# Two-phase MoE routing on one TensorE core: the search split from the gathering of its rows, and stated two experts ahead

## The chip, the cores and the metric

The kernel runs on one core of a Trainium2 chip. The metric is the device time of one execution, in microseconds, the median of several runs; lower is better. The profile below is of one execution. Engines by their names in the profile: PE is the matrix engine (PEld its weight loads), DVE the vector engine, ACT the scalar engine, POOL the GpSimd engine, SP the queue that issues plain DMAs.

## What is computed

A windowed attention (4 batches, 8 heads, 576 positions, 64 dimensions a head) gives 2304 tokens of 512 values. Two mixture-of-experts layers follow, each with 8 experts of 512 x 1024 x 512. The first weighs all experts for each token. The second gives each expert at most `cap` = 288 tokens, greedily by logit, and this case is about it:

```python
logits = x @ w_gate
flat = logits.flatten()
order = np.argsort(-flat)
for idx in order:
    tok, e = (int(idx) // E, int(idx) % E)
    if assigned[tok] >= 0 or counts[e] >= cap:
        continue
    assigned[tok] = e
    counts[e] += 1
for e in range(E):
    mask = assigned == e
    h = np.maximum(x[mask] @ w1[e], 0.0)
    out[mask] = h @ w2[e]
```

## The kernel before

The attention and the first layer fill some 1590 us under an order written out by hand. The last 320 us are the second layer, and they lie outside that: a scheduler places each instruction on its engine's queue, by the order in which the code states it (earlier is more urgent) and by its own guess of durations. Each engine then runs its queue strictly in that order, so a wrong guess becomes a wait.

The second layer runs in eight phases, one for each expert in the order in which experts fill up. `route(ph)` (L1102) finds the phase's expert and tokens. Its search is a radix search for the logit at which the first expert is full: six rounds, each a comparison `G` on DVE (L1143, L1145), a histogram of 18 small matmuls (L1149), two short DVE reductions (`f8`, `fl`, L1151 and L1152) and one to three matmuls that broadcast the digit (L1156, `bs`). After it come the counts (L1168), the expert's index and the index `widx` of its weights (L1182), and the state that the next search needs: `ob`, `cap`, `un` (L1240 to L1246). Prefix sums give each token its slot (`tot`, L1211; prefix matmuls L1214 and L1216; `sl`, `jv`). One-hot rows `oh` and `rh` (L1230, L1234) and the index matmul (L1238, 18 matmuls) turn slots into the list of token rows `idx` (L1250). POOL gathers those rows from `xrows` in three parts of 96 (L1255), and the expert's weights in four parts of 1 MB (L1190). PE transposes the rows (L1274, three times 8), into `xgt`. The last phase has no radix search.

`ffn(ph)` (L1285) is the expert: 8 first-layer tiles of 12 matmuls with 288 columns each (L1299), evicted as `hh` on ACT (L1301) and `hl` on DVE (L1302), from two PSUM buffers, so a tile can start when the tile two before it has been evicted by both; then 4 second-layer tiles of 24 matmuls (L1311), evicted as `yT` (L1313). `put(ph)` (L1315) turns `yT` back (L1321), copies it on ACT into one of two tiles `tmp` (L1323) and scatters it to the output from POOL (L1325); its three parts stand inside the first layer of the next phase.

`second()` states the work in this order: the search and rows of phase 0, the rest of the first layer, then for each phase the whole of `route(ph + 1)` and `ffn(ph)`:

```python
bg.start("route", route_all())
for ph in range(E):
    bg.until(("r", min(ph + 1, E - 1)))
    ffn(ph, before)
    before = put(ph)
```

So `route(ph + 1)` runs inside `ffn(ph)`: its search beside the first layer, its rows and transposes beside the second. The tiles of a route have one buffer each, but for `widx` (2), `wp` (2), `idx` (3) and `sv` (3). The weights have two sets of buffers, used in turn, the gathered rows `xgb` six tiles, and `xgt` two.

## Time and profile before

| | us |
|---|---|
| median of 3 runs | 1925.43 |
| lowest and highest run | 1922.45, 1926.74 |
| time of the profiled execution | 1916.18 |
| its span, from first to last instruction | 1914.4 |
| PE busy in the span | 1845.1 |
| DVE busy | 1242.6 |
| ACT busy | 889.8 |
| POOL busy | 107.7 |

The profiled execution is 9.25 us shorter than the median of the runs. Busy time of PE holds the drain of each matmul, which overlaps the next one. A phase of the second layer is read from one first-layer start of `ffn` to the next: phase 0 from 1636.9 us, then 1665.8, 1700.9, 1735.95, 1771.0, 1806.0, 1841.0 and 1866.5. A wait is idle time of an engine just before an instruction, with what released it.

### The profile page before, as it was taken

How to read it: one execution, taken by the hardware profiler on the slowest of the kernel's cores; microseconds unless marked ns; L12 is line 12 of the kernel's file. 1: busy time of each engine (PE TensorE's matmuls, PEld its weight loads, DVE VectorE, ACT ScalarE, POOL GpSimd, SP SyncE). 2: the span in 40 equal slices, each digit the busy share in tenths (PEclk: the TensorE clock that was granted, in tenths of full speed). 3: DMA queues.
4: the chain of work that ended last, by engine and by line, in shares of the span. 5: the costliest groups of instructions: out<-in, count | busy, mean ns of one | idle time of the engine just before them, and what ended most of it. 6: DMA issues, size and time to landing. Idle time of an engine off the chain costs nothing.

```text
span 1914.4 us, 40759 instructions
## 1 busy us (share of the span) xinstructions
PE 1845.1 (96%) x16205; PEld 1319.9 (69%) x16205; DVE 1242.6 (65%) x3808; ACT 889.8 (46%) x2439; POOL 107.7 (6%) x140
## 2 busy tenths in 40 slices
PE   6999999999999999999999999999999998999987
PEld 5877555777676676767766867677677774667765
DVE  7777956664666666676667666766757767565540
ACT  6666334543455545555554555455534442222222
POOL 0000000000000000000000000000000102323231
PEclk8999999999999999999999999999999999899999
DMA  8573022320324225234351343234231111535451
GB/s 191 111 156 75 1 89 72 105 89 1 111 80 164 89 95 167 93 109 127 118 165 67 122 136 130 94 101 159 89 105 27 36 29 62 185 121 177 163 210 30
DMA packets 172799, 203.40 MB, mean 106 GB/s; under 512 B 83000, under 2 KB 130104, under 8 KB 168512
## 3 DMA queue, kind: packets, MB, share of 16 engines
q1 hardware_dynamic: 164928, 157.78, 27.1%
q0 software_dynamic: 7680, 43.02, 6.4%
q8 instruction: 127, 2.08, 0.4%
q14 instruction: 64, 0.52, 0.1%
HBM read 143.05 MB, written 57.71 MB: 105 GB/s over the span
## 4 chain that ended last, share of the span: by engine, by line
PE 74%; DVE 9%; DMA 7%; issue 5%; ACT 3%; POOL 1%; SPq 0%; POOLq 0%; ACTq 0%; DVEq 0%
PE p L940 27%; PE p L862 17%; PE pb L862 12%; PE p L770 4%; PE p L1299 4%; DMA ws<-st2k 2%; DMA raw<-in_moe_w_dram 2%; DVE st2k L347 1%; DMA raw<-xrows,idx 1%; PE pb L630 1%; DMA w2scr<-st2k 1%; PE pb L1149 1%; PE p L1311 1%; ACT st2k L345 1%; PE pb L617 1%
## 5 line engine op out<-in xcount | busy, mean ns | idle before, releaser
L940 PE MATMUL p<-w2b,hh 128*128 128x512 f16 x2304 | 686.1, 379 | 0.0
L940 PE MATMUL p<-w2b,hl 128*128 128x512 f16 x1152 | 436.6, 379 | 0.0
L940 PEld LDWEIGHTS <-hh 128*128 128x128 f16 x2304 | 221.6, 99 | 218.2 <-issue 0.7
L862 PEld LDWEIGHTS <-w1b 128*128 128x128 f16 x4032 | 340.3, 98 | 22.9 <-issue 4.2
L862 PEld LDWEIGHTS <-w1x 128*128 128x128 f16 x3024 | 256.2, 98 | 19.7 <-issue 5.9
L862 PE MATMUL p<-th,w1x 128*128 128x192 f16 x1344 | 221.3, 246 | 3.1 <-ACT sa L874 2.4
L862 PE MATMUL pb<-xh,w1b 128*128 128x192 f16 x1344 | 221.3, 246 | 0.0
L940 PEld LDWEIGHTS <-hl 128*128 128x128 f16 x1152 | 112.6, 98 | 135.4 <-issue 0.5
L862 PE MATMUL pb<-xl,w1b 128*128 128x192 f16 x672 | 165.3, 246 | 0.0
L862 PE MATMUL p<-tl,w1x 128*128 128x192 f16 x672 | 165.3, 246 | 0.0
L347 DVE SCALAR_TENSOR_TENSOR st2k<-raw,wsc,st2k 128x512 f16<-128x512 f32 x128 | 92.1, 748 | 49.9 <-ACT st2k L345 49.6
L956 DVE SCALAR_TENSOR_TENSOR acc<-p,SE,acc 128x512 f32<-128x512 f32 x126 | 94.0, 746 | 40.2 <-PE p L940 39.9
L345 ACT ACTIVATE st2k<-raw,wsc 128x512 f16<-128x512 f32 x128 | 87.0, 714 | 69.1 <-DMA ws<-st2k 54.8
L862 PE MATMUL p<-th,w1b 128*128 128x192 f16 x672 | 110.6, 246 | 3.0 <-ACT sc L895 2.9
L743 ACT ACTIVATE hh<-sb 128x192 f16<-128x192 f32 x168 | 61.0, 363 | 112.5 <-DVE sb L906 112.5
L1005 POOL TENSOR_TENSOR st2k<-tmp,st2k 128x512 f16<-128x512 f32 x18 | 24.5, 1361 | 1575.5 <-ACT tmp L1003 1554.6
L862 PE MATMUL pb<-xh,w1x 128*128 128x192 f16 x672 | 110.6, 246 | 0.0
L862 PE MATMUL p<-xh,w1b 128*128 128x192 f16 x672 | 110.6, 246 | 0.0
L743 ACT ACTIVATE hh<-sa 128x192 f16<-128x192 f32 x168 | 60.9, 363 | 106.4 <-DVE sa L880 106.4
L295 ACT ACTIVATE st2k<-raw 128x512 f16<-128x512 f32 x116 | 72.3, 624 | 80.4 <-DMA raw<-in_moe_w_dram 52.0
L744 DVE SCALAR_TENSOR_TENSOR hl<-sa,hh 128x192 f16<-128x192 f32 x168 | 60.2, 358 | 72.1 <-ACT hh L743 72.1
L744 DVE SCALAR_TENSOR_TENSOR hl<-sb,hh 128x192 f16<-128x192 f32 x168 | 60.1, 358 | 71.7 <-ACT hh L743 71.7
(308 smaller groups left out, 3280.9 us busy)
## 6 DMA issues: line engine op xcount, KB each, us to landing
raw<-in_moe_w_dram SPq DMA_DIRECT2D x128, 512.0 KB, 5.5
ws<-st2k SPq DMA_DIRECT2D x128, 256.0 KB, 4.4
w2b<-w2scr SPq DMA_DIRECT2D x28, 512.0 KB, 6.4
w2scr<-st2k SPq DMA_DIRECT2D x48, 256.0 KB, 4.3
xrows<-st2k SPq DMA_DIRECT2D x18, 257.0 KB, 3.1
vs<-in_v_dram SPq DMA_DIRECT2D x35, 128.0 KB, 4.1
ldq<-in_q_dram SPq DMA_DIRECT2D x16, 256.0 KB, 4.5
ldk<-in_k_dram SPq DMA_DIRECT2D x16, 256.0 KB, 4.8
```

The lines of the kernel that those rows point to most:

```text
L295: A.activation(junk[:, 0:512], s0, AF.Square, accum_out=mp[:, c:c + 1])
L345: A.activation(hi, src, AF.Copy, scale=sc)
L347: V.scalar_tensor_tensor(lo, src, sc, hi, op0=OP.mult, op1=OP.subtract)
L617: PE.transpose(pp[:, hp], pn[:, b, hp], ident)
L743: A.activation(hh[:, f, cols], src, AF.Relu)
L744: V.scalar_tensor_tensor(hl[:, f, cols], src, 0.0, hh[:, f, cols], op0=OP.max, op1=OP.subtract)
L770: PE.matmul(p[:, 0:w], w1v[wi][:, c, fs], x[:, c, ts], start=(n == 0), stop=(n == 3 * DC - 1))
L862: PE.matmul(bank[:, 0:HB], aq[wi][:, c, fs], xq[xi][:, c], start=(start and n == 0), stop=(n == 5), skip_group_check=True)
L940: PE.matmul(p, h[:, f, js], w2v[wi][:, f], start=(n == 0), stop=(n == 3 * FC - 1))
L956: V.scalar_tensor_tensor(acc[:, i], p, SE[:, e, i:i + 1], acc[:, i], op0=OP.mult, op1=OP.add)
L1005: G.tensor_tensor(xr[:, DM:2 * DM], xs, xr[:, 0:DM], OP.subtract)
L1299: PE.matmul(p[:, 0:CAP], wv1[f // 4][w][:, c, fs], xt[:, x * DC + c], start=(n == 0), stop=(n == 3 * DC - 1))
```

## The change

`route(ph)` now ends with the state: it no longer asks for weights and no longer builds `oh`, `rh`, `idx`, but states `ob`, `cap`, `un` and `wp` and returns a second generator, `rows_of(ph)`, with the slots `sl` and `jv` in hand. `rows_of` asks for the first half of the weights, builds `oh`, `ohj` and `rh`, runs the index matmul, gathers the rows, asks for the other half, and transposes. `weave(ph, b)` runs the search of phase `ph` and, from its second step on, one step of the rows part `b` of the phase before after each step of the search; what is left of `b` follows. Before `ffn(ph)` the code now states the search of `ph + 2` woven with the rows of `ph + 1`. `widx` and `wp` get three buffers, `sl` and `jv` two.

```diff
-        widx = rt([128, 1], "widx", I32, bufs=2)
+        widx = rt([128, 1], "widx", I32, bufs=3)
...
-        gather(*((0, x) for x in range(1 if ph == 0 else 2)))
...
-        sl = rt([128, NT], "sl")
+        sl = rt([128, NT], "sl", bufs=2)
...
-        oh = rc["oh"]
-        V.tensor_tensor(oh, ...)
-        ohj = rt([128, NT, NJ], "ohj")
-        V.tensor_tensor(ohj, ...)
-        rh = rt([128, NT, NJ, 2], "rh", F16)
-        V.tensor_tensor(rh, ...)
-        yield 1
-        pi = rc["psr"].tile([128, 512], F32, name="pb")
-        for t in range(NT):
-            PE.matmul(pi[0:R, 0:2 * NJ], oh[:, t], rh[:, t].rearrange("p j x -> p (j x)"), ...)
...
+        wp = rt([128, 1], "wp", bufs=3)
+        V.tensor_tensor(wp, wv[:, 0:1], wv[:, 1:2], OP.mult)
+        return rows_of(ph, last, sl, jv, wp, ws, widx)
+
+    def rows_of(ph, last, sl, jv, wp, ws, widx):
...
+        gather(*((0, x) for x in range(1 if ph == 0 else 2)))
+        oh = rc["oh"]
+        V.tensor_tensor(oh, ...)
+        ohj = rt([128, NT, NJ], "ohj")
+        V.tensor_tensor(ohj, ...)
+        rh = rt([128, NT, NJ, 2], "rh", F16)
+        yield 1
+        V.tensor_tensor(rh, ...)
+        yield 1
+        pi = rc["psr"].tile([128, 512], F32, name="pb")
+        for t in range(NT):
+            PE.matmul(pi[0:R, 0:2 * NJ], oh[:, t], rh[:, t].rearrange("p j x -> p (j x)"), ...)
...
+        def weave(ph, b):
+
+            a = route(ph)
+            n = 0
+            while True:
+                try:
+                    next(a)
+                except StopIteration as x:
+                    a = x.value
+                    break
+                n += 1
+                if b is not None and n > 1:
+                    next(b, None)
+            for _ in b or ():
+                pass
+            return a
...
+        b = weave(1, b)
         before = iter(())
         for ph in range(E):
-            bg.until(("r", min(ph + 1, E - 1)))
+            if ph + 2 < E:
+                b = weave(ph + 2, b)
+            elif b is not None:
+                for _ in b:
+                    pass
+                b = None
             ffn(ph, before)
```

In the new file lines 1205, 1207, 1251, 1256, 1260, 1264, 1269, 1246, 1282, 1307, 1309, 1310, 1319, 1321, 1329, 1331 and 1333 are what 1214, 1216, 1230, 1234, 1238, 1250, 1255, 1190, 1274, 1299, 1301, 1302, 1311, 1313, 1321, 1323 and 1325 were.

The first place is POOL's queue in phase 2, from the gather of the rows of phase 3 on. `raw` are the gathered rows, `w2b` and `xh` weight buffers, `out_0_dram` the output; the `idx` of a store tells its phase. Before (the rows of phase 3 are `idx_22166`, the stores of phase 1 `idx_21070`):

```order
L1325 DMA out_0_dram<-tmp_3046,idx_21070 2304x512 x3
L1190 DMA w1b_83<-ws00_120,widx_22105 128x4096
L1190 DMA w1b_83<-ws01_121,widx_22105 128x4096
L1255 DMA raw_78<-xrows_129,idx_22166 96x1028 x3
L1190 DMA w2b_84<-ws10_122,widx_22105 128x4096
L1190 DMA w2b_84<-ws11_123,widx_22105 128x4096
```

and now (the rows of phase 3 are `idx_22245`, the stores of phase 1 `idx_21149`):

```order
L1269 DMA raw_78<-xrows_129,idx_22245 96x1028 x3
L1246 DMA w2b_84<-ws10_122,widx_21857 128x4096
L1246 DMA w2b_84<-ws11_123,widx_21857 128x4096
L1333 DMA out_0_dram<-tmp_3046,idx_21149 2304x512 x3
L1246 DMA xh_75<-ws00_120,widx_22417 128x4096
L1246 DMA xh_75<-ws01_121,widx_22417 128x4096
```

The stores, which stood first in the phase, stand behind the row gathers and the second half of the weights, and the first half of the weights is that of phase 4 (`xh`) and not of phase 3.

The second place is ACT's queue in phase 2: `hh` are evictions of the first layer, `tmp` the three output copies of `put(1)`, `xgt` evictions of the row transposes. Before:

```order
L1301 ACTIVATE hh0_79<-p1_22213 128x288
L1323 ACTIVATE tmp_3046<-p2_22228,sv_21083 96x512
L1301 ACTIVATE hh0_79<-p1_22236 128x288
L1323 ACTIVATE tmp_3046<-p2_22251,sv_21083 96x512
L1301 ACTIVATE hh0_79<-p1_22259 128x288
L1323 ACTIVATE tmp_3046<-p2_22274,sv_21083 96x512
L1301 ACTIVATE hh0_79<-p1_22282 128x288
L1301 ACTIVATE hh0_79<-p1_22297 128x288
```

and now:

```order
L1331 ACTIVATE tmp_3046<-p2_22494,sv_21161 96x512
L1286 ACTIVATE xgt1_20238<-pb_22283 128x8x96
L1286 ACTIVATE xgt1_20238<-pb_22335 128x8x96
L1309 ACTIVATE hh0_79<-p1_22502 128x288
L1309 ACTIVATE hh0_79<-p1_22525 128x288
L1309 ACTIVATE hh0_79<-p1_22540 128x288
L1309 ACTIVATE hh0_79<-p1_22555 128x288
L1331 ACTIVATE tmp_3046<-p2_22517,sv_21161 96x512
L1309 ACTIVATE hh0_79<-p1_22570 128x288
L1309 ACTIVATE hh0_79<-p1_22585 128x288
```

The third output copy, which followed the third `hh`, follows the sixth, with two more behind it, and the evictions of the row transposes come into the first layer.

The third place is DVE's queue in phase 0, at the end of the search of phase 1: `oh` is the one-hot of the rows of phase 1, `un` and `hm` belong to the next search. Before (`p1_21162` is the fourth first-layer tile):

```order
L1302 SCALAR_TENSOR_TENSOR hl0_80<-p1_21162,hh0_79 128x288
L1228 SCALAR_TENSOR_TENSOR sl_21028<-jv_21034,sl_21028 128x18
L1232 TENSOR_TENSOR ohj_21039<-jv_21034,j3_20077 128x54
L1230 TENSOR_TENSOR oh_20240<-i96_20075,sl_21028 128x1728
L1234 TENSOR_TENSOR rh_21041<-ohj_21039,tp_20079 128x108
L1246 SCALAR_TENSOR_TENSOR un_20098<-s2_21030,un_20098 128x18
L1302 SCALAR_TENSOR_TENSOR hl0_80<-p1_21177,hh0_79 128x288
```

and now (`p1_21390` is the third tile, `p1_21405` the fourth):

```order
L1227 SCALAR_TENSOR_TENSOR un_20098<-s2_21028,un_20098 128x18
L1130 TENSOR_SCALAR mi_21063<-mi_21063 128x18
L1251 TENSOR_TENSOR oh_20240<-i96_20075,sl_21026 128x1728
L1132 SCALAR_TENSOR_TENSOR hm_21067<-sx_21061,un_20098 128x18
L1253 TENSOR_TENSOR ohj_21098<-jv_21032,j3_20077 128x54
L1133 TENSOR_SCALAR hm_21067<-hm_21067 128x18
L1310 SCALAR_TENSOR_TENSOR hl0_80<-p1_21390,hh0_79 128x288
L1143 TENSOR_TENSOR G_21071<-hm_21067,cj_20067 128x720
L1256 TENSOR_TENSOR rh_21100<-ohj_21098,tp_20079 128x108
L1310 SCALAR_TENSOR_TENSOR hl0_80<-p1_21405,hh0_79 128x288
```

The `hl` of the third and fourth tile stand behind `oh`, and the first `G` of the search of phase 2 with them.

On PE the row transposes and the index matmul of phase `ph + 1` stand in the first layer of `ffn(ph)`; they stood in its second layer.

## Rows read from the trace of the kernel before

**Rows 1.** Windows: length, busy us (count) of PE, PEld, DVE, ACT, POOL; PEclk; DMA

```profile
1636.90:1665.80 28.90, 28.05 (x241) 21.08 (x239) 14.73 (x66) 6.04 (x13) 6.90 (x7) 0.94 0.67 244
...
1735.95:1771.00 35.05, 33.46 (x372) 24.91 (x371) 21.19 (x83) 8.61 (x17) 9.85 (x10) 1.00 0.44 154
...
1841.00:1866.50 25.50, 22.27 (x187) 17.60 (x185) 7.76 (x21) 6.69 (x13) 7.46 (x8) 0.87 0.75 267
```

**Rows 2.** PE waits (us, times, longest): phase 3, then phases 0, 1, 5, 6

```profile
PE pb L1274 <- DMA raw<-xrows,idx: 1.1, 3, 0.4
PE pb L1238 <- DVE rh L1234: 0.3, 1, 0.3
PE pb L1214 <- DVE tot L1211: 0.2, 1, 0.2
...
PE pb L1274 <- DMA raw<-xrows,idx: 0.7, 2, 0.4
...
PE pb L1274 <- DMA raw<-xrows,idx: 2.0, 3, 1.2
...
PE pb L1274 <- DMA raw<-xrows,idx: 1.3, 3, 0.7
...
PE pb L1274 <- DMA raw<-xrows,idx: 3.0, 1, 3.0
```

**Rows 3.** PE timeline, end of phase 6's wait: start, us, line, op, count, [idle]

```profile
1855.88 0.82 PE L1274 MATMUL pb<-id,raw 96*128 96x96 f16 x8 [2.96 <-DMA raw<-xrows,idx]
1856.49 0.92 PE L1299 MATMUL p<-xgt,xh 128*128 128x288 f16 x3
...
1859.21 4.46 PE L1299 MATMUL p<-xgt,xh 128*128 128x288 f16 x24
```

**Rows 4.** PE timeline, phase 3

```profile
1744.91 0.60 PE L1321 MATMUL p<-ident,yT 128*96 128x128 f32 x4
1745.48 0.61 PE L1149 MATMUL pb<-A,G 128*40 128x8 f16 x18
1746.02 0.79 PE L1299 MATMUL p<-xgt,w1b 128*128 128x288 f16 x5
...
1762.14 0.97 PE L1238 MATMUL pb<-rh,oh 128*96 128x6 f16 x18 [0.30 <-DVE rh L1234]
...
1767.17 0.51 PE L1274 MATMUL pb<-id,raw 96*128 96x96 f16 x8 [0.36 <-DMA raw<-xrows,idx]
1767.53 0.29 PE L1311 MATMUL p<-hh,w2b 128*128 128x288 f16 x1
```

**Rows 5.** PE timeline, phase 0, after the prefix matmuls

```profile
1643.99 4.11 PE L1299 MATMUL p<-xgt,xh 128*128 128x288 f16 x32
```

**Rows 6.** POOL timeline, phase 3

```profile
1741.47 1.41 POOL L1325 DMA_INDIRECT out_dram<-tmp,idx  x1 [6.57 <-ACT tmp L1323]
1744.44 0.93 POOL L1325 DMA_INDIRECT out_dram<-tmp,idx  x1 [1.56 <-ACT tmp L1323]
...
1764.08 0.92 POOL L1255 DMA_INDIRECT raw<-xrows,idx  x1 [5.46 <-DVE idx L1250]
1765.31 0.92 POOL L1255 DMA_INDIRECT raw<-xrows,idx  x1 [0.30 <-issue]
```

**Rows 7.** DVE timeline, phase 3

```profile
1741.10 0.97 DVE L1145 SCALAR_TENSOR_TENSOR G<-hm,pb,cj 128x720 f16<-128x720 f32 x1 [0.57 <-PE pb L1156]
...
1763.65 0.16 DVE L1250 SCALAR_TENSOR_TENSOR idx<-ti 96x3 int32<-96x3 f32 x1
```

**Rows 8.** DVE timeline, phase 0

```profile
1645.97 0.45 DVE L1302 SCALAR_TENSOR_TENSOR hl<-p,hh 128x288 f16<-128x288 f32 x1
...
1646.54 1.95 DVE L1230 TENSOR_TENSOR oh<-i,sl 128x1728 f16<-128x1728 f16 x1
```

**Rows 9.** DMA issues from 1600 us on: count, KB each, median us to landing

```profile
out_dram<-tmp,idx POOLq DMA_INDIRECT x24, 2.7
...
w2b<-ws,widx POOLq DMA_INDIRECT x8, 8.1
```

More of the change, by code (lines that the diff above doesn't have):

```diff
@@ L1223, in route @@
             V.tensor_tensor(sl, sl, s2, OP.add)
-        jv = rt([128, NT], "jv")
+        jv = rt([128, NT], "jv", bufs=2)
         V.tensor_scalar(jv, sl, float(R), None, op0=OP.is_gt)
@@ L1246, in route, with rt, gather @@
             V.scalar_tensor_tensor(rc["un"], s2, 0.0, rc["un"], op0=OP.is_equal, op1=OP.mult)
+        wi = rt([128, 2, E], "wi")
+        wv = rt([128, 2], "wv")
+        V.tensor_tensor(wi, winv[:, 2:4], bc(eo[:, None, :], [128, 2, E]), OP.mult)
+        V.tensor_reduce(wv, wi, AX.X, OP.add)
+        wp = rt([128, 1], "wp", bufs=3)
+        V.tensor_tensor(wp, wv[:, 0:1], wv[:, 1:2], OP.mult)
+        return rows_of(ph, last, sl, jv, wp, ws, widx)
+    def rows_of(ph, last, sl, jv, wp, ws, widx):
+        def rt(shape, name, dt=F32, bufs=1):
+            return rc["rpool"].tile(shape, dt, name=name, bufs=bufs)
+        def gather(*parts):
+            with ExitStack() as st:
+                if "lastx" in rc:
+                    st.enter_context(tc.issue_after(rc["lastx"]))
+                for m, a in parts:
+                    G.indirect_dma_start(out=ws[m][:, a * 4096:(a + 1) * 4096], out_offset=None, in_=wscr[m][a],
+                                         in_offset=bass.IndirectOffsetOnAxis(ap=widx[:, :1], axis=0))
+        gather(*((0, x) for x in range(1 if ph == 0 else 2)))
+        oh = rc["oh"]
+        V.tensor_tensor(oh, bc(rc["i96"][:, None, :], [128, NT, R]), bc(sl[:, :, None], [128, NT, R]), OP.is_equal)
+        ohj = rt([128, NT, NJ], "ohj")
+        V.tensor_tensor(ohj, bc(jv[:, :, None], [128, NT, NJ]), bc(rc["j3"][:, None, :], [128, NT, NJ]), OP.is_equal)
+        rh = rt([128, NT, NJ, 2], "rh", F16)
+        yield 1
+        V.tensor_tensor(rh, bc(ohj[:, :, :, None], [128, NT, NJ, 2]), bc(rc["tp"][:, :, None, :], [128, NT, NJ, 2]), OP.mult)
+        yield 1
+        pi = rc["psr"].tile([128, 512], F32, name="pb")
+        for t in range(NT):
+            PE.matmul(pi[0:R, 0:2 * NJ], oh[:, t], rh[:, t].rearrange("p j x -> p (j x)"), start=(t == 0), stop=(t == NT - 1))
         ti = rt([R, NJ, 2], "ti")
@@ L1348, in second @@
             rc[n] = late.enter_context(tc.tile_pool(name=n, bufs=x, space=PSUM))
-        first = route(0)
-        for x in first:
+        def weave(ph, b):
[13 more added lines that the diff above has]
+            return a
+        b = weave(0, None)
+        for x in b:
             if x == "rows":
@@ L1354, in second @@
         rest()
-        def route_all():
-            for ph in range(E):
-                for _ in first if ph == 0 else route(ph):
-                    yield 1
-                bg.done.add(("r", ph))
-                yield 1
-        bg.start("route", route_all())
+        b = weave(1, b)
         before = iter(())
         for ph in range(E):
-            bg.until(("r", min(ph + 1, E - 1)))
+            if ph + 2 < E:
[4 more added lines that the diff above has]
+                b = None
             ffn(ph, before)
```

17 lines of the change are left out of this document (removed).

## Prediction

> **What bounds the kernel now.** I call the work between two first-layer starts of `ffn` phase 0 to 7. I read the trace in this order: the busy time by phase, the waits of PE in each phase, then the timelines of PE, POOL and DVE round those waits. [rows 1] In a middle phase PE is busy 33.46 of 35.05 us at full clock, DVE 21.19, POOL 9.85. So TensorE is the bound, and the same matmuls run in any order: an edit that moves no PE work out of the program can gain only PE's idle time. [rows 2] That is 1.1 + 0.3 + 0.2 = 1.6 us in phase 3, and phases 2 and 4 look the same; the transposes of the gathered rows (L1274) wait for their gather, the index matmul (L1238) for `rh`, the prefix matmul (L1214) for `tot`. The last two repeat in phases 1 and 5, the 0.3 in 6. Phase 0 has 0.7, phase 1 has 2.0 + 0.5 = 2.5, phase 5 has 1.3 + 0.5 = 1.8, phase 6 has 3.0 + 0.3 = 3.3.
>
> [...] All that can be won from phase 0 on is then 0.7 + 2.5 + 4.8 + 1.8 + 3.3 + 3.1 = 16.2 us.
>
> The stretch before phase 0 idles more, but there the order on PE and POOL stays as it is until the first L1299, so I count it at nothing.
>
> **The change part by part.** It adds no matmul and takes none away. `wp` and the three tiles with more buffers cost no instruction. The index and gather lines move from the end of a search into the next phase's first layer.
>
> *Phases 2 to 4: waits on `tot` and `rh`.* The prefix matmul stands in the second layer behind 30 first-layer matmuls, and `oh` and `rh` are made while the second layer runs, a third of a phase before the index matmul. Both waits go: 0.5 in each.
>
> *Phases 2 to 4: the wait on the gather.* Units, from start to start in [rows 4]: four `yT` transposes 0.57, a histogram of 18 matmuls 0.54, eight row transposes 0.36; a first-layer matmul 0.123, and an L1156 no more than that. From the end of the index matmul to the first transposes the new order has 19 first-layer matmuls, 7 `yT` transposes, one histogram and 5 L1156: 2.35 + 1.0 + 0.55 + 0.6, with switches about 4.6 us. The gather needs `ti` and `idx`, about 0.5 on DVE (0.7 in [rows 4, 7], where a `G` stands between), 0.27 from `idx` to POOL, and 3.09 from its start on POOL to the transposes [rows 4, 6, 7]: 3.9. The next two gathers start 1.22 apart [rows 6]. But it now starts while DVE runs the search's `G`, which it did not. [rows 6, 7] The store of 1741.47, which began 0.37 after a `G`, took 1.41 on POOL; the next, which began with none running, 0.93. I take 0.48 more for the first gather, and all three land that much later: 4.35, 5.57, 6.8 after the index matmul. PE asks at 4.6, then (eight transposes, two matmuls) at 5.25, then (eight transposes, a histogram, one matmul, after the 0.3 it waited) at 6.6. Waits 0 + 0.3 + 0.2 = 0.5 against 1.6.
>
> [...]
>
> *Phase 1* starts its index matmul 2.2 us later, with a fuller DVE: the same count gives 0.3 + 0.5 + 0.3 = 1.1 against 2.5.
>
> *Phases 5 and 6.* No full search is left, so less stands between the index matmul (now first in the phase) and the transposes: 12 + 9 matmuls and 4 `yT` transposes, 3.15 us, against 3.86 for the gather (no `G` beside it). Waits 0.7 + 0.5 + 0.4 = 1.6 in each, against 1.8 and 3.3. None is long, and three waits of this kind within 3 us left the clock full in phase 3 [rows 1, 2]: I take the 3.1 of lower clock as gone.
>
> *Phase 0 pays.* It takes over the second search's histograms, which phase 1 gives up: nothing by itself. But DVE's order there changes. `oh` starts at 1646.54 and holds DVE 1.9 us [rows 8]. Before, the `hl` of the third first-layer tile ran ahead of it; now it stands behind it and three short ones. That tile's PSUM buffer is what the fifth first-layer tile writes, so PE waits for it. PE: before, 32 first-layer matmuls follow the prefix matmuls from 1643.99 [rows 5]; now the prefix matmuls come two matmuls sooner, at 1643.7, and 23 matmuls, 2.8 us, stand between them and the fifth tile: it asks at 1646.5. DVE: `oh` starts no earlier (two more short ones ahead of it, one `hl` fewer), ends at 1648.4, then the short ones, 0.15, and the `hl` of 0.45 [rows 8]: 1649.0. A stall of 2.4 us, 1.9 to 3.0. The row gathers of that phase come out at 1.2, against 0.7.
>
> *Nothing at all:* the first-layer weights of the next phase but one are asked for when their buffer is free, a phase ahead (landing 8.1 us, [rows 9]); the index tile with three buffers waits for stores of two phases ago; the `sv` reads on DVE, which now stand inside the search, wait for the third gather and put the next step back 0.3, which PE covers with two matmuls and a `yT` transpose; without that cover it is 0.3 a phase.
>
> **Sum.** Before 16.2. After: phase 0 2.4 + 1.2, phase 1 1.1, phases 2 to 4 3 x 0.5, phases 5 and 6 2 x 1.6: 9.4. Gain 6.8, less 0.2 for the extra switches of PE between kinds of matmul: 6.6. The profiled execution goes from 1914.4 to 1907.8 of span, from 1916.18 to 1909.6 of time; the median of the runs lies 9.25 above that execution, and I carry the difference over: 1925.43 - 6.6 = **1918.8**, say 1919. About 0.2% (3.9 us) is what a measurement of this kernel can tell from no change.
>
> **Rivals.**
>
> [...]
>
> 2. *The gather waits stay.* PE's place for the transposes is fixed in the program; if the gathers land 0.3 later than I count, each of the three waits keeps its 0.3 in phases 1 to 4, a loss of 0.9 x 4 = 3.6: 1922.5. For it: in phase 1 before, one such wait was 1.2 [rows 2]. Against: no weights are in flight beside them any more.
>
> 3. *The stores fall behind the weights (slower).* In phases 2 to 6 the stores of the phase before stand on POOL behind three row gathers and two weight gathers. The third output copy on ACT needs the tile of the first store, and two `hh` of the first layer stand behind that copy on ACT. The first gather starts 4.6 us into the phase (3.8 for PE up to the end of the index matmul, 0.8 as above), and five issues of some 1.24 later store 0 starts, at 10.8. If it is not held up it lands 2.7 later [rows 9], at 13.5; if it lands with the weight gather issued at 9.6 (8.1 to land), at 18 to 19. The `hh` is wanted by the second layer at 22.9, so the copy may end as late as 22. It costs only if two such landings come one after the other, 9.6 + 16.2 + 2.7 = 28.5: 6 us in each of four phases, 24 - 6.6 more than before: 1943.
>
> [...]
>
> **How the numbers follow.** Forecast (1916.5 to 1921.5) 0.50; rivals 1 and 2 together 0.32, of which a third still ends under 1921.6; rival 4 0.08; rival 3 or another mishap of its sign 0.10. Faster by over 0.2%: 0.50 + 0.08 + 0.10 = 0.68; slower 0.10; within 0.2% 0.22. The range takes in rivals 1, 2 and 4, with the spread of the three medians' runs (3 below, 1.3 above): 1912 to 1925.5.
>
> **What would show it.** Right: in phases 2 to 4 no PE wait on `tot` or `rh`, and under 0.7 on the gathers; phase 6 without a 3 us wait, and the clock full there; in phase 0 one wait of about 2.4 on the DVE's `hl`, just before the fifth first-layer tile; phase 0 some 5 + 3 us longer, phases 5 and 6 shorter by as much as the search that they no longer hold. Wrong: a PE wait on ACT or on DVE inside the first layers of phases 2 to 4, ACT waiting for `out_dram`, a granted clock under 0.9 in phase 0, or transposes that still wait 1 us.

## The result: 1.3% slower on the recorded pair, level on two other chips

| | before | after |
|---|---|---|
| median of 4 runs each | 1923.94 us | 1947.27 us |
| lowest and highest run after | | 1944.66, 1949.49 us |
| ratio after to before, 95% interval | | 1.0129 (1.0102 to 1.0156) |
| time and span of the profiled execution | 1916.18, 1914.4 us | 1944.66, 1942.8 us |

Three of the four runs of before are those of the table ahead. The forecast was 1919 us and faster. The profile after, by phases 0, 3 and 6 (start to start of the first layer; columns as in [rows 1]):

```profile
1639.77:1680.29 40.52, 36.27 (x365) 26.00 (x364) 28.56 (x131) 6.02 (x13) 9.15 (x9) 0.90 0.48 176
1761.79:1802.00 40.21, 35.78 (x373) 26.66 (x371) 20.48 (x83) 8.37 (x17) 9.96 (x10) 0.92 0.39 135
1874.67:1903.93 29.26, 26.64 (x233) 20.89 (x231) 4.73 (x14) 7.62 (x16) 7.43 (x8) 1.00 0.34 113
```

A middle phase takes 40.2 us where it took 35.05 [rows 1], with the same matmuls. (The phase starts given ahead for the kernel before lie up to 1.45 us early: the first L1299 of phase 3 stands at 1737.40, not 1735.95. A middle phase is 35.06 us long by either, but phase 1 is 36.0 us and not 35.1.) PE's granted clock is 0.92 there: 1.00 up to 1773.8 us, 0.55 from there to 1778.0 and 0.50 in the 2 us after. PE's waits in phase 3 (us, times, longest) are not those of [rows 2]:

```profile
PE pb L1149 <- DVE G L1143: 2.0, 1, 2.0
PE pb L1149 <- issue: 1.1, 2, 0.5
PE pb L1156 <- issue: 0.5, 1, 0.5
PE pb L1282 <- issue: 0.5, 1, 0.5
PE pb L1282 <- ACT xgt L1286: 0.2, 1, 0.2
```

No wait on the gather, on `tot` or on `rh`. PE waits for the search's own `G`, and for nothing that the profile shows ("issue"). Why `G` is late stands on DVE. First PE's timeline of that stretch (start, us, line, count, [idle before]), then DVE's, then ACT's:

```profile
1767.30 0.61 PE L1149 MATMUL pb<-A,G 128*40 128x8 f16 x18
1769.06 0.16 PE L1156 MATMUL pb<-fl,sw 40*128 40x1 f16 x1 [0.47 <-issue]
...
1773.88 0.64 PE L1149 MATMUL pb<-A,G 128*40 128x8 f16 x10 [1.99 <-DVE G L1143]
1775.03 0.17 PE L1149 MATMUL pb<-A,G 128*40 128x8 f16 x1 [0.51 <-issue]
```

```profile
1768.66 0.16 DVE L1151 TENSOR_TENSOR f<-pb,cap 40x8 f32<-40x8 f32 x1 [1.49 <-PE p L1329]
...
1772.19 0.24 DVE L1160 TENSOR_SCALAR k<-hm,pb 128x18 f32<-128x18 f32 x1 [3.19 <-PE pb L1282]
...
1775.94 0.56 DVE L1284 COPY xgt<-pb 128x768 f16<-128x768 f16 x1 [1.99 <-remote]
```

```profile
1770.08 0.41 ACT L1309 ACTIVATE hh<-p 128x288 f16<-128x288 f32 x1 [3.55 <-PE p L1329]
```

The histogram of 1767.30 ended at 1767.91, but `f`, which reads it, starts 0.75 us later with DVE idle. The L1156 matmul of 1769.06 ended at 1769.22; `k`, which needs it, starts at 1772.19, 3.0 later; the `G` for which PE waits is made from `k`. The releasers that the profile names for them (L1329, L1282, "remote") are then only the last events that it has, not what the step waited for. In the trace of before the same two steps start 0.04 us behind their matmuls, as most do elsewhere in this trace (phase 3 of before, PE and then DVE):

```profile
1742.19 0.61 PE L1149 MATMUL pb<-A,G 128*40 128x8 f16 x18
1743.82 0.17 PE L1156 MATMUL pb<-fl,sw 40*128 40x1 f16 x1
```

```profile
1742.84 0.16 DVE L1151 TENSOR_TENSOR f<-pb,cap 40x8 f32<-40x8 f32 x1 [0.76 <-PE pb L1149]
...
1744.03 0.24 DVE L1160 TENSOR_SCALAR k<-hm,pb 128x18 f32<-128x18 f32 x1 [0.60 <-PE pb L1156]
```

I call this **late signals**: a step starts up to microseconds behind the end of the matmul that releases it, with its engine idle, as if the event came late. Only steps that wait for PE are so; DVE's `G` ends at 1773.82, and PE starts 0.06 us later. The same places are late in all middle phases, and PE stalls inside one histogram, as at 1775.03. The DMA view has a second mark of it: no time to landing for POOL's transfers, which [rows 9] had.

```profile
raw<-xrows,idx POOLq DMA_INDIRECT x24
out_dram<-tmp,idx POOLq DMA_INDIRECT x24
```

The weight gathers on that queue have none either. So the trace lacks landings of just POOL's queue, and signals are late while its row gathers run.

### The profile page after: what moved, and what is told of

It is laid out like the page before. It is cut to its first block, busy times and chain, and to the rows that moved or that the text cites. A ratio compares the mean times of both kernels' runs of the same rounds, so it can differ in the third digit from the quotient of the medians.

```text
span 1942.8 us, 40770 instructions
## 1 busy us (share of the span) xinstructions
PE 1853.8 (95%) x16205; PEld 1326.1 (68%) x16205; DVE 1239.4 (64%) x3808; ACT 887.7 (46%) x2439; POOL 109.5 (6%) x140
## 3 DMA queue, kind: packets, MB, share of 16 engines
q8 instruction: 127, 2.08, 0.4%
## 4 chain that ended last, share of the span: by engine, by line
PE 77%; DVE 9%; issue 5%; DMA 4%; ACT 3%; POOL 1%; another core or an unknown queue 1%; SPq 0%; POOLq 0%; ACTq 0%; DVEq 0%
PE p L940 30%; PE p L862 17%; PE pb L862 12%; PE p L770 4%; PE p L1307 3%; PE p L1319 3%; PE pb L1149 1%; DMA raw<-in_moe_w_dram 1%; DMA w2scr<-st2k 1%; PE pb L630 1%; DVE st2k L347 1%; PE pb L617 1%; PE pb L988 1%; PE pb L588 1%; DMA ws<-st2k 1%
## 5 line engine op out<-in xcount | busy, mean ns | idle before, releaser
L770 PE MATMUL p<-xh,w1b 128*128 128x384 f16 (+1 forms) x512 | 101.2, 288 | 6.0 <-DVE hl L752 5.8
```

What stands on the lines that cost most here:

```text
L770: PE.matmul(p[:, 0:w], w1v[wi][:, c, fs], x[:, c, ts], start=(n == 0), stop=(n == 3 * DC - 1))
```

## The experiments

Each run stands beside the kernel before on the same chip. The recorded pair's chip is not named. The runs fell on seven chips, each met on one occasion only, and on two of these, 0 and 13, signals were late.

| run | chip | median us | ratio to before, 95% interval |
|---|---|---|---|
| a_again, after unchanged | 4 | 1917.85 | 1.0011 (0.9992 to 1.0031) |
| a_third, after unchanged | 2 | 1920.78 | 1.0010 (0.9995 to 1.0026) |
| **a_fourth, after unchanged** | **0** | **1951.85** | **1.0111 (1.0084 to 1.0139)** |
| b_again, before unchanged | 15 | 1916.19 | 0.9996 (0.9985 to 1.0008) |
| b_bufs | 4 | 1913.78 | 0.9989 (0.9977 to 1.0001) |
| **b_shift64** | **0** | **1919.17** | **0.9949 (0.9925 to 0.9974)** |
| a_shift64 | 2 | 1910.14 | 0.9956 (0.9938 to 0.9973) |
| **a_shift128** | **0** | **1950.76** | **1.0109 (1.0084 to 1.0135)** |
| **a_shift64_oh** | **0** | **1948.79** | **1.0087 (1.0061 to 1.0113)** |
| a_shift64_oh2, the same | 11 | 1907.63 | 0.9954 (0.9938 to 0.9969) |
| rows_last | 4 | 1935.32 | 1.0095 (1.0078 to 1.0111) |
| rows_first | 4 | 1911.62 | 0.9985 (0.9970 to 1.0000) |
| rf_again, the same | 15 | 1913.98 | 0.9981 (0.9969 to 0.9993) |
| **rf_third, the same** | **13** | **1940.20** | **1.0084 (1.0060 to 1.0108)** |
| rf_shift64 | 1 | 1911.44 | 0.9974 (0.9964 to 0.9985) |
| a_svlate | 2 | 1922.74 | 1.0027 (1.0011 to 1.0042) |
| rf_svlate | 2 | 1915.48 | 0.9989 (0.9977 to 1.0001) |
| a_noxr | 15 | 1905.24 | 0.9943 (0.9923 to 0.9962) |

The rows in bold ran where signals were late. The kernel before itself took 1915.0 to 1918.1 on chips 1, 2, 4, 11 and 15, and 1928.9 and 1925.5 on 0 and 13. A theory's letter holds inside its own expectation.

### The program or the chip

Two theories for the late signals: they belong to the program (its order, or the addresses that the extra buffers moved), or to the load (the program as it was put on one chip at one time). The changed kernel again, without an edit, and the kernel before with the extra buffers alone:

```diff
+ widx, wp: bufs=3; sl, jv: bufs=2     (in the kernel before, nothing else)
```

> The changed kernel once more, for a second trace. In its first trace DVE and ACT start up to 5.2 us after the matmul that they wait for has ended (0.04 us everywhere else and in the kernel before), in a stretch of 8 us behind each row gather of phases 1 to 5, and PE then waits 2 to 5 us in the search and runs at the lower clock for some 5 us. Theory A, the late signals belong to the program: the same lags at the same places (0.75, 1.8, 2.3 to 3.0, 5.2 us in phases 3 to 5), time 1942 to 1950. Rival C, they are an accident of one load or one chip: other lags or none, and a time under 1935.

> The kernel before with the added buffers alone (widx and wp three, sl and jv two), which move the addresses of the tiles behind them and nothing else. Theory A (the late signals come from the search's steps standing beside the row gathers): as before, within 0.3%, no lag over 0.1 us behind the row gathers. Rival C (addresses or the program's place in memory make them): lags at the row gathers of phase 0, where the instructions of both kernels are the same and the changed one already shows 0.7 to 2.6 us, and 5 to 25 us slower.

> The changed kernel unchanged, a third time. Its first trace had late signals from PE behind the row gathers (up to 5.2 us) and was 1.3% slower than the kernel before; its second had none and was level with it (1917.9 against 1916.4). Theory C, the late signals belong to one load or one chip and not to the program: either kind may come, and with it the time: level within 0.3% without them, 1942 to 1950 with them. Theory A (they belong to the program) expects them each time and is already against the second trace.

> The changed kernel, unaltered, on one more load. If the late signals of the recorded run (k L1160 starting 3.0 us behind the end of its matmul in every middle phase, 1944.7 us) belong to the program, they are here again: 1942 to 1950. If they belong to that load or chip, as two loads without them suggest: 1914 to 1925 with every such lag at 0.04 us.

> The kernel before, unaltered, with a profile of its own on this load. If this load is of the kind that made PE's signals late under the changed kernel (a fourth of them: 1951.9 us against 1928.9 of before), theory L (during the row gathers' transfers the core's signals arrive late; the search's round trips between PE and DVE pay for it where they stand in that stretch) expects: the late starts are here too, but only at the two xgt copies behind the gathers, 2 to 2.5 us behind their transposes, with the search's k and f steps at 0.2 us or less, and middle phases of 35.0 to 35.5 us, 1917 to 1930 us in all. Rival A (the changed kernel alone makes signals late): no start later than 0.1 us and the gathers' landings complete in the record. On a load of the other kind: both at 1914 to 1920 with no late start.

On chips 4 and 2 the changed kernel is level with the kernel before, and no signal is late. In a_again, phase 3, the steps that were late stand so on DVE:

```profile
1750.12 0.16 DVE L1151 TENSOR_TENSOR f<-pb,cap 40x8 f32<-40x8 f32 x1 [0.78 <-PE pb L1149]
...
1750.92 0.24 DVE L1160 TENSOR_SCALAR k<-hm,pb 128x18 f32<-128x18 f32 x1 [0.45 <-PE pb L1156]
```

`k` starts 0.80 after `f`. In a_fourth, the same program on chip 0, 2.93 after it (phase 2):

```profile
1732.92 0.16 DVE L1151 TENSOR_TENSOR f<-pb,cap 40x8 f32<-40x8 f32 x1 [1.52 <-PE p L1329]
...
1735.85 0.24 DVE L1160 TENSOR_SCALAR k<-hm,pb 128x18 f32<-128x18 f32 x1 [2.58 <-PE pb L1282]
...
1740.32 0.56 DVE L1284 COPY xgt<-pb 128x768 f16<-128x768 f16 x1 [2.71 <-remote]
```

with ACT's `hh` between them, and ACT's copy of the row transposes 5.3 us behind those, which ended at 1734.93:

```profile
1734.36 0.41 ACT L1309 ACTIVATE hh<-p 128x288 f16<-128x288 f32 x1 [3.60 <-PE p L1329]
...
1740.21 0.81 ACT L1286 ACTIVATE xgt<-pb 128x768 f16<-128x768 f16 x1 [3.60 <-remote]
```

```profile
1734.42 0.51 PE L1282 MATMUL pb<-id,raw 96*128 96x96 f16 x8
```

Where signals are late, they come to DVE and ACT in bursts: here at 1732.92, 1734.36, 1735.85 and 1740.2, in phase 3 of the recorded trace at 1768.66, 1770.08, 1772.19 and 1775.84, so with no one spacing. That goes from about 2 us after the first row gather begins on POOL (1730.09 in this phase, 1765.86 in the other) to some 10 us after; behind the start of a store at 1683.41 us of the recorded trace, with no row gather near, an `f` starts 0.35 and a `G` 0.20 us behind the end of its matmuls. All four traces from chip 0 show it, and no trace from chips 1, 2, 4, 11 and 15. So it is the chip, or the occasion, that makes signals late: no chip was met twice, and these two were not told apart. The program decides what that costs: 1.1% here, by an order that is level elsewhere. Addresses alone do not make signals late, since a_again and a_fourth are one program; and b_shift64 (below) has late signals without the extra buffers. b_bufs ran where nothing was late, and shows only that the buffers cost nothing there.

### What late signals cost in the order before

The kernel before with 64 tiny matmuls in its first microseconds (meant for the next section) fell on chip 0, and is the only trace of the order before from such a chip.

```diff
+ for _ in range(64):
+     PE.matmul(pp[0:2, 0:2], pad, pad, start=True, stop=True)
```

> The kernel before with the same 64 tiny matmuls (128 PE instructions). If theory E is right the gain of 0.5% with 64 in the changed kernel belongs to the meeting of its gathers with the fetch: the kernel before, whose middle phases show no gather landing 4.5 us after its issue, stays within 0.2% of itself (ratio 0.998 to 1.002), and the changed kernel with the shift is then faster than the kernel before by the change itself. Rival: the shift alone is worth 0.4 to 0.5% in any kernel: ratio 0.995 to 0.996, and the change is worth nothing.

Its ratio is the rival's, and the kernel before left no trace on that chip to set beside it. What its trace does show is where late signals fall (its line numbers are 5 higher than before's): phase 3, and from the end of phase 2 DVE's copy of the row transposes and PE's first histogram of the next search.

```profile
1741.74:1776.94 35.20, 33.47 (x373) 24.92 (x370) 21.09 (x83) 8.67 (x18) 9.86 (x10) 1.00 0.45 156
```

```profile
1740.60 0.56 DVE L1281 COPY xgt<-pb 128x768 f16<-128x768 f16 x1 [2.77 <-PE p L1316]
```

```profile
1741.19 0.61 PE L1154 MATMUL pb<-A,G 128*40 128x8 f16 x18
```

The copy starts 2.4 us behind its transposes, which end at 1738.20. But the copy is wanted by the next phase's first layer only, so nobody waits, and a phase takes 35.2 us at full clock, as in [rows 1]. The search starts at 1741.19, when the gathers are over. In the changed kernel the search's rounds, in which PE, DVE and PE wait for each other in turn, stand in that very stretch. From the start of phase 0 to the end a_fourth takes 309.5 us against 280.8 in a_again, 28.7 more; b_shift64 takes 283.4 against 275.8 in b_again, 7.5 more: 4.5, 4.4 and 2.1 in phases 0, 5 and 6 (in 0 and 6 PE does wait for ACT's copy of the transposes, 2.0 and 3.4 us), less 3.4 in phase 1, which is the fetch's (below). The difference, 21 us, is 1.1%. These are single executions on four loads, so the 21 us are an estimate.

The next runs were to test that with the search behind the rows:

```diff
-                b = weave(ph + 2, b)
+                for _ in b:
+                    pass
+                b = weave(ph + 2, None)
```

> The run of before with the next phase's rows stated whole ahead of the search two phases ahead (1911.6 us, ratio 0.9985, where signals were on time). On a load with late signals theory L expects it level with the kernel before, 0.995 to 1.003, since its search's round trips stand behind the row gathers as they do before, with k starting within 0.5 us of its matmul's end; the interleaving of the rows with the search is then what costs the changed kernel its 1.1 to 1.3% on such a load. Rival P (going two phases ahead costs by itself there): 1.008 to 1.014. On a load of the other kind: 0.997 to 1.000 again.

> The next phase's rows stated whole ahead of the search two phases ahead, on one more load. If its signals are late (landings of POOL's queue missing from the record): theory L, 0.995 to 1.003 of before with k starting within 0.5 us of its matmul's end; rival P, 1.008 to 1.014. If its signals are on time: 0.997 to 1.000 as in the two runs so far, which then stand as one result over three loads.

rf_again fell on a chip without late signals and repeats rows_first. rf_third fell on chip 13, and its 1.0084 is the rival's number. The trace says why my number was wrong. Phase 3, and DVE in it:

```profile
1761.12:1799.97 38.85, 34.89 (x373) 26.47 (x371) 21.09 (x83) 8.49 (x17) 9.75 (x10) 0.96 0.40 140
```

```profile
1764.81 0.16 DVE L1151 TENSOR_TENSOR f<-pb,cap 40x8 f32<-40x8 f32 x1 [1.91 <-PE p L1307]
...
1767.01 0.97 DVE L1145 SCALAR_TENSOR_TENSOR G<-hm,pb,cj 128x720 f16<-128x720 f32 x1 [1.55 <-PE pb L1282]
```

Stated behind the rows, the search still does not run behind them: its second round's `f` and third round's `G` fall beside the gathers and start 1.2 and 1.4 us behind their matmuls, which ended at 1763.62 and 1765.61. `k`, which I had named, falls after the stretch and is on time. So the run had not the property that it was to test. What it shows is that the same order loses 5.5 us a phase against rf_again (38.85 against 33.33), with all of PE's longer waits in the stretch of late signals. That the rival (going two phases ahead costs by itself) is wrong is supported by the 0.998 of that order elsewhere, not by a run that separates the two on such a chip.

Which transfers make signals late was the question of a_noxr: the changed kernel without the row gathers of phases 2 to 7, which work on rows gathered by phases 0 and 1.

```diff
+            if ph < 2:
                 xd = G.indirect_dma_start(out=x, ...)
```

> The changed kernel without the row gathers of phases 2 to 7 (they work on rows that phases 0 and 1 gathered; the rest of the work, the weight gathers and the stores stay). On a load with late signals, theory R (the row gathers' transfers make them late): no late start of f, k, hh or xgt in the phases from the third on, phases 2 to 5 at 33 to 34 us where the changed kernel has 40 to 42, 1915 to 1925 in all. Rival W (the weight gathers or the stores of POOL's queue make them late): late starts of 2 us and more stay in phases 2 to 5 and it stays over 1935. On a load of the other kind: the gather waits of phases 2 to 6 and the half clock behind them go, 1902 to 1909.

It fell on a chip without late signals, so the run does not answer it. The trace of the recorded pair answers a part: later in phase 3, with no row gather near them, a store (1787.76) and both weight gathers start on POOL, and ACT's evictions of the second layer stay 2.94 us apart, the first of them 0.04 us behind its matmuls.

```profile
1789.20 1.21 POOL L1246 DMA_INDIRECT w1b<-ws,widx  x1 [0.30 <-issue]
1790.72 1.10 POOL L1246 DMA_INDIRECT w1b<-ws,widx  x1 [0.30 <-issue]
```

```profile
1792.75 0.41 ACT L1321 ACTIVATE yT<-p 128x288 f32<-128x288 f32 x1 [2.89 <-PE p L1319]
1795.69 0.41 ACT L1321 ACTIVATE yT<-p 128x288 f32<-128x288 f32 x1 [2.53 <-PE p L1319]
```

So weight gathers alone do not make signals late; that row gathers alone do is not shown. a_noxr gives a price instead, the middle phase with no row gather at all:

```profile
1746.79:1779.84 33.05, 33.00 (x375) 25.53 (x373) 20.68 (x84) 8.61 (x18) 7.14 (x7) 1.00 0.42 146
```

PE is busy 33.00 of 33.05 us: on such chips everything that the changed order still loses in middle phases is the gathers' waits and the clock behind them. 1905 us, with no row gather from phase 2 on, is about its floor.

### PE's instruction fetch in the gather's way

Where signals were on time, phases 2 to 4 had one gather wait of 0.7 to 1.8 us each, where I had forecast small ones of 0.5 in all. a_again, phase 3: POOL's second row gather, PE, and the DMA traffic between 1750.9 and 1752.6 us (the row of a queue: packets, MB, share of 16 engines).

```profile
1749.26 0.92 POOL L1269 DMA_INDIRECT raw<-xrows,idx  x1 [0.30 <-issue]
```

```profile
1753.89 0.51 PE L1282 MATMUL pb<-id,raw 96*128 96x96 f16 x8 [1.33 <-DMA raw<-xrows,idx]
```

```profile
q8 instruction: 1, 0.02, 4.9%
```

The gather took 4.6 us from issue to use where the median of this trace's 24 row gathers is 3.1 us to landing; 15 of its 16 landings came by 1752.32, the last at 1753.85. q8 carries instructions, in pieces of 16 KB (its row for the whole execution of a_again: 127 packets, 2.08 MB). That they are PE's is my inference: PE has 32410 instructions with its weight loads, and 2.08 MB over these is 64 bytes each. Here one piece goes through amid the gather's packets (4.9% of 16 engines over 1.7 us is 1.3 us of one engine). In each of the phases 2 to 4 of a_again, a_third and a_svlate a fetch starts 2.6 to 5.4 us behind the first gather. The kernel before has the same once, in phase 1: a fetch starts 4.1 us behind the first gather of its profiled execution (4.8 in b_again), the third gather is used 4.0 (5.0) us after its issue, and PE waits 1.2 (2.2) us for it. To move the fetch, I put 64 tiny matmuls (128 PE instructions with their weight loads, half a piece) into the first microseconds; with 128 of them a whole piece, so that the fetch should fall back where it was.

> The changed kernel with 64 tiny extra matmuls (128 instructions with their weight loads) on PE in the first 5 us, while it waits for its first input; they write nothing that is read. In the second trace of the changed kernel a 16 KB instruction fetch of PE (queue q8) started at 1751.1, among the packets of the second row gather of phase 3, one of the 16 engines landed that gather 1.5 us after the other 15, and PE waited 1.3 for it; phases 2 and 4 have the same. Theory E (the fetch holds up that one engine's rows): the extra instructions move the fetch half a page, some 5 us in that stretch, out of the gathers of phases 2 to 4; the waits there fall from 1.3 to 1.5 to under 0.5 each, the 3.4 us of lower clock in phase 4 go, and the time is 4 to 6 us less than the changed kernel's, 1911 to 1914 where the changed one has 1918. Rival F (the gather is late for another reason, such as the G beside it): waits of 1.3 stay and the time is the changed kernel's within 2 us.

> The changed kernel with 128 tiny matmuls in its first microseconds (256 PE instructions, one whole 16 KB page of them, where the run with 64 had half a page); their outcome is used by nothing. Theory E (PE's 16 KB instruction fetch falls amid the row gather's packets and holds its last landing): with a whole page added the fetch falls back where it was among the instructions, so the gather waits of phases 2 to 4 return at 1.2 to 1.5 us each, with half clock behind one or two of them: 1916 to 1922 us, level with the unchanged changed kernel. Rival (the tiny matmuls help by something else, such as an earlier clock or a later start of PE): no gather wait over 0.4 us in phases 2 to 4 and 1909 to 1912 us, as with 64.

> The next phase's rows stated whole ahead of the search two phases ahead, and 64 tiny matmuls (half a page of PE instructions) in the first microseconds. On a load with signals on time: theory E gives no more here, since with the rows whole the middle phases already show gather waits of 0.2 to 0.3 us, so it is level with the rows stated whole alone (0.998 to 1.000 of before); rival: the shift is worth its 0.5% in any order of statement, 0.993 to 0.995. On a load with late signals theory L (the search's round trips pay where they stand beside the row gathers) gives 0.990 to 1.003 of before with k starting within 0.5 us of its matmul's end; rival P (going two phases ahead costs by itself there) 1.006 to 1.014.

a_shift64: 10.6 us less than a_third on the same chip. Between the two traces 8.2 us lie from phase 0 on: 2.9 in phase 0, 7.1 in phases 2 to 4, and 1.7 lost again in 5 and 6; 2.5 us lie ahead of phase 0, where the fetch theory names nothing. No gather wait in phases 0 to 4, no fetch in the 5 us behind a first gather in phases 1 to 4, and the phase is near a_noxr's floor:

```profile
1740.54:1773.71 33.17, 33.03 (x373) 25.32 (x371) 20.59 (x83) 8.41 (x17) 10.70 (x10) 1.00 0.47 164
```

a_shift64_oh2 (below) repeats that on another chip. a_shift128 fell on chip 0, where late signals cover what it was to show: its fetches are back, 2.6 and 2.9 us behind the first gathers of phases 2 and 3, but its time says nothing on them, and the rival (the tiny matmuls help by something else) is not excluded by a run. rf_shift64 gains nothing over rows_first and rf_again beyond their intervals, as expected: that order has no such wait to lose. b_shift64's 0.5% on chip 0 speaks against "it is worth nothing in the order before". A part of it is the fetch of phase 1, which moved to 1.2 us ahead of the first gather: the phase takes 35.1 us at full clock where b_again has 38.5 at 0.96. The rest is not explained. The order before with the 64 matmuls did not run on a chip without late signals, so it is not shown that the changed order adds anything to them.

PE itself has no wait of the kind "issue" in phases 0 to 6 of a_again; what the fetch costs there is the gather's, 1.5 us of landing.

### The wide comparison beside POOL

Phase 5 had gather waits of 2.9 us where 1.6 were forecast. a_again, POOL and then DVE at its start:

```profile
1815.68 2.63 POOL L1269 DMA_INDIRECT raw<-xrows,idx  x1 [11.19 <-DVE ohj L1253]
1818.61 0.92 POOL L1269 DMA_INDIRECT raw<-xrows,idx  x1 [0.30 <-issue]
```

```profile
1815.56 1.95 DVE L1251 TENSOR_TENSOR oh<-i,sl 128x1728 f16<-128x1728 f16 x1
```

The first gather begins 0.12 us after the last phase's `oh`, an instruction with two SBUF inputs, and takes 2.63 us instead of 0.92: it ends 0.8 after `oh` does. A weight gather that begins at 1751.70, 0.06 behind a `G` of 0.91 us with two SBUF inputs (L1143), takes 1.68 and ends 0.8 after it. In rows_last (below) the second gather of phase 3 begins 0.36 us after an `oh` and takes 2.40. Where the gather began first it was not held (0.92 at 1748.03 in phase 3, with a `G` from 1748.37). The edit queues that `oh` behind the three `sv` products on DVE, on top of a_shift64:

```diff
+            if last:
+                st.enter_context(tc.issue_after(rc["lastsv"]))
             V.tensor_tensor(oh, ...)
```

> The run with 64 tiny matmuls, and in the last phase's rows the wide one-hot comparison (L1251 of the changed kernel, 1.95 us of DVE) is queued on DVE behind the three sv products of the rows before, so it no longer runs while POOL begins phase 5's first row gather. Theory (a POOL DMA issue that begins while a wide DVE instruction with two SBUF inputs runs is held until that ends): the first gather of phase 5 takes 0.9 to 1.0 us on POOL instead of 2.6, PE's gather wait there falls from 2.5 to 0.6 to 1.0 us and its half clock of some 3.4 us goes: 2 to 3.5 us less than with 64 alone, 1906.5 to 1908.5. Rival (the first gather is late by something else, the fetch or its own list): it still takes 2.6 us and the time stays at 1909 to 1911.

> The run with 64 tiny matmuls and the last phase's wide one-hot comparison behind the three sv products, once more, since its first run fell on the load with late signals. On a load with signals on time: the first row gather of phase 5 at 0.9 to 1.0 us on POOL, PE's wait there at 0.6 to 1.2 us and its half clock gone, 1906 to 1909 us or 0.993 to 0.996 of before (0.9956 with the 64 alone); rival (the wait there is the landing's, whoever issues it): 1909 to 1912, 0.995 to 0.997. On a load with late signals: 1.006 to 1.012 again.

The first gather of phase 5 takes 0.93 on chip 0 and 0.92 on chip 11:

```profile
1806.86 0.92 POOL L1277 DMA_INDIRECT raw<-xrows,idx  x1 [10.82 <-DVE ohj L1261]
...
1813.04 2.62 POOL L1342 DMA_INDIRECT out_dram<-tmp,idx  x1 [0.31 <-issue]
```

```profile
1812.91 1.94 DVE L1259 TENSOR_TENSOR oh<-i,sl 128x1728 f16<-128x1728 f16 x1
```

Phase 5 goes from 33.0 to 30.2 us with the clock full, as forecast. But the moved `oh` now holds a store, and phase 6 grows from 29.6 to 32.3, with an `hl` wait of 2.6 and a clock of 0.95; that the store is the reason is not shown. The ratio is a_shift64's. What held the gather is shown; the time gained by it is not.

### The rows' place, and the `sv` products

rows_last states the search two phases ahead whole and the rows behind it; rows_first the other way round (its diff stands above).

```diff
-                b = weave(ph + 2, b)
+                nb = weave(ph + 2, None)
+                for _ in b:
+                    pass
+                b = nb
```

> The changed kernel with the weaving undone inside the loop: the search of two phases ahead is stated whole, and the rows part of the next phase behind it, so that rows, gathers and transposes come after the search's rounds again while the search stays two phases ahead. Theory A: no histogram stands beside a row gather any more, so the lags go, the clock stays full, 1915 to 1928. Rival B (the search two phases ahead is what costs, by the later stores, weights and copies): 1940 to 1950 still. Rival C: lags stay behind the gathers, over 1935.

> The changed kernel with the rows part stated whole ahead of the search of two phases ahead: index matmul, gathers and transposes first in the phase, the search behind them in urgency but at the same time where its own chain lets it. Theory A: the histograms still run while the gathers are in flight, so the lags stay, perhaps shorter by what the first rounds lose: 1935 to 1950, PE idle 3 to 5 us in phases 2 to 4. Rival D (it is the sv reads and transposes queued inside the search on DVE and PE that hold it up, not the late signals): the search no longer has them between its steps, so the wait for G falls under 0.5 us and the time under 1928.

rows_last misses the numbers of A and B, and has the time of C without its lags (no late signal): its gathers start late in the phase, the second one beside an `oh`, PE waits 2.6 us for them in phase 3, its clock is 0.95, and the phase is 37.7 long. On this chip neither theory of rows_first could be told from the other, since nothing was late. rows_first is the best order of the three without any shift, with gather waits of 0.2 to 0.3 in phases 2 to 4.

In phases 5 and 6 of a_again PE waits 0.8 and 2.2 us for `hl`. I held the `sv` products, which wait for gathers ahead of it on DVE, responsible, and moved them behind the transposes:

```diff
-        sv = ... ; three V.tensor_tensor(sv[:, j:j + 1], ...)   (ahead of the transposes)
+        the same, behind them
```

> The changed kernel with the three sv products (L1276) stated behind the row transposes instead of ahead of them. In its second trace the hl of the first layer stands on DVE behind the sv of the third row gather in phases 5 and 6, and PE waits 0.8 and 2.2 for that hl. Theory G (that queue place makes the waits): both go, 2 to 3 us less than the changed kernel; phases 2 to 4 gain 0 to 0.3 each. Rival H (the xgt copy, which waits for the second transposes, holds hl as long): waits and time stay within 1 us.

> The version with the rows part stated whole ahead of the search (0.15% faster than the kernel before, interval 0 to 0.3%), with the sv products behind the transposes as well. Theory G: its hl waits of 0.3 and 0.9 in phases 5 and 6 go, and sv no longer stands ahead of a G: 1 to 2.5 us less than that version, 0.2 to 0.3% faster than the kernel before. Rival H: as that version within 1 us.

The waits of a_svlate stay (1.4 and 1.6 us; a_third, without the edit, has 0.3 and 1.4), and nothing is gained. The theory fell. These waits also change from trace to trace of one program (rows_first 0.4 and 0.9, rf_again none), so that rf_svlate has none says nothing. DVE's copy `xgt`, which also waits for a gather and stands ahead of `hl`, would hold it as long; that was not tried apart.

## Why the prediction was wrong, point by point

**The size on the recorded pair.** The step that failed is "Phases 2 to 4: the wait on the gather". It counted the histogram and the L1156 between the index matmul and the transposes as work that PE runs through, and so gave the signals between PE and DVE no time, as the trace of before shows them (0.04 us). On the chip of the recorded pair the change put the search's rounds, which live on those signals, beside the row gathers, where they came up to 5 us late: phases 1 to 4 take 22.5 us more than in a_again, the same program with signals on time. No part of the sum and no rival had it. Rival 3 had a loss of that size by another mechanism, stores behind weights, and that did not come: ACT waits for no store in phases 0 to 4.

**The constant.** I carried the 9.25 us between the profiled execution and the median over as if it were spread. The kernel before takes 1915 to 1918 us on chips without late signals and 1925 to 1929 with them; 1925.43 fits the second kind, and the profile, with all its landings, the first. That fits, but the first median's chip is not known.

**Where signals are on time,** the forecast of 6.6 us less was still wrong: level, 1.0011 and 1.0010. That 1917.85 and 1920.78 us lie near the 1919 is luck, since the kernel before takes 1916.36 and 1917.77 on these chips. Against a_again:

| phase | forecast idle and clock, us | measured |
|---|---|---|
| 0 | 2.4 `hl` + 1.2 gathers | 2.1 + 0.7 + 0.2, and a clock of 0.89 (0.94 before) |
| 1 | 1.1 | 0.5 |
| 2, 3, 4 | 0.5 each | 1.5 each, and in phase 4 a clock of 0.95 |
| 5 | 1.6 | 2.9 + 0.8 `hl`, clock 0.95 |
| 6 | 1.6 | 1.5 + 2.2 `hl` |

```profile
1635.75:1675.02 39.27, 36.17 (x366) 25.82 (x365) 28.54 (x131) 6.02 (x13) 8.58 (x9) 0.89 0.55 198
...
1743.97:1778.56 34.59, 33.05 (x373) 25.34 (x371) 20.70 (x83) 8.48 (x17) 10.87 (x10) 1.00 0.46 157
1778.56:1814.88 36.32, 34.66 (x375) 26.45 (x372) 21.36 (x94) 8.37 (x17) 10.68 (x10) 0.95 0.44 150
```

PE's idle time in these phases is 15.4 us where the sum had 9.4, and the lower clock, which the sum had at nothing, comes on top.

- Right: the waits on `tot` and `rh` go, but for 0.2; phase 0 pays a wait on `hl` just before the fifth first-layer tile, 2.1 for 2.4; PE's work is the same; phase 6's 3 us wait goes. The last is no proof of the change: in b_again, the kernel before once more, phase 6 waits 1.3 us at full clock, and the long wait (3.0 in all, clock 0.96) stands in phase 1.
- "Phases 2 to 4: the wait on the gather": the count of units was right, since with the fetch moved no gather wait is left. The fetch was not in it: it adds 1.5 us to the second gather of phase 3 in a_again. It was one row of the page's DMA queues, and I had priced no other traffic in the gather's 3.09. The 1.2 us wait of phase 1 that rival 2 cites was such a case.
- The 0.48 for a `G` beside POOL: right in kind and put at the wrong place. In phase 3 the gather began first. The instruction that holds a gather was `oh` in phase 5, for which I wrote "no `G` beside it". The gather took 2.63 us beside it, and 0.93 and 0.92 with `oh` moved.
- Phases 5 and 6: the `hl` waits were missed; `xgt` and `sv` now stand ahead of `hl` on DVE and wait for gathers.
- "I take the 3.1 of lower clock as gone": gone from phase 6, but back in phases 4 and 5 behind gather waits of 1.5 and 2.4 us, and in phase 3 of a_third (0.91) behind one of 1.3. In phase 0 the clock stayed full behind the 2.1 us for `hl` and fell at 1661 behind the gather's 0.7 (two L1319 in a row take 0.25 us at 1643.24 and 0.43 at 1661.15). So the length of the wait alone does not tell when the clock falls. As a term of the sum the 3.1 was an estimate of mine, a time that no run shows. What the trace of before shows behind phase 6's wait [rows 3] is a granted clock of 0.50 from 1855.8 to 1861.0 us and 0.75 from there to 1863.0, with PE busy for 7.12 of those 7.20 us; the missing clock adds up to 2.6 + 0.5 us. Rival 2, waits on the gather that stay, came true, by the fetch.

**What stays open.** What makes signals late on chips 0 and 13: the traces show that POOL's landings are missing there and that PE's signals come in bursts, not why. Nor is it known whether it stays with the chip.

## What to carry to other kernels

Before a 1% change is called good or bad, time it on several chips and look for steps that start microseconds behind their matmul: an order that puts round trips between engines beside indirect gathers lost 1.1% where signals were late and was level elsewhere. If a gather lands 1.5 us late, look for an instruction fetch amid its packets, and move it by half a piece of dummy instructions before you touch the order (64 tiny matmuls: 1910.14 us against 1920.78 on chip 2). Let POOL's issue of an indirect DMA begin ahead of a wide DVE instruction with two SBUF inputs, not behind its start (0.92 us against 2.63 in a_again). Of what was tried, the changed order with 64 tiny matmuls was fastest on chips without late signals (0.995 to 0.996 of before; the order before with them was not tried there), and the order before loses least on the others.

## What the runs showed of the hardware that I had not expected

- On two of seven chips (and in the recorded trace) PE's signals reach DVE and ACT up to 5.3 us late (a_fourth, ACT's `xgt`), in bursts, while POOL's row gathers run; on the other five `k` starts 0.04 us behind its matmul.
- PE's fetch of 16 KB of instructions, some 1.3 us of one DMA engine, goes with a last landing of a gather 1.5 us late (a_again, phase 3: 4.6 us for 3.1); with the fetch moved by 64 tiny matmuls that wait is gone on two chips.
- An indirect DMA that begins on POOL during a DVE instruction of 1.95 us with two SBUF inputs takes 2.6 us instead of 0.92; one that began 0.34 us ahead of a `G` of 0.97 us took 0.92. Which property of the instruction counts was not tried.
